# Attention, routed experts and a rational feed-forward on one core: expert stores without mutual waits, a branch hint for ScalarE, the conversion steps dealt out anew, the router's last part in another order

## The chip, the cores and the metric

The kernel runs on 1 core of a Trainium2 chip. The metric is device time in microseconds (us). Engines: TensorE (PE; PEld is its weight load), VectorE (DVE), ScalarE (ACT), GpSimd (POOL) and SyncE (SP), which only issues transfers here. Each takes its instructions in program order.

## The reference

- Chunked attention on q, k, v (4 batches, 8 heads, 768 positions, 64 wide): each chunk of 32 positions sees 8 memory keys, 16 positions to the left and 8 to the right. The result is x, 3072 tokens x 512.
- A mixture of experts: `logits = x @ w_gate + modality_bias[modality_id]`; each token goes to its best expert of 8; `out = gate * (relu(x @ w1[e]) @ w2[e])`, with 512 x 1024 and 1024 x 512 weights.
- A feed-forward stage: `h = x @ w_in` (2048 wide), `g = P(h) / (Q(h) + 1e-6)` with a cubic P and `Q = 1 + |b0||h| + |b1|h^2`, then `g @ w_out`.

All is float32; w_in, w_out, a and b arrive as float64.

## The kernel before, in words

Three stages follow each other on the PE. Attention (`attention`) walks 24 tiles of 128 tokens, writes x to a DRAM tensor `xd` and ends in `Router.second`. The experts (`moe`) work on units of 128 tokens of one expert: units 0, 1 and 2 (`EARLY`) one by one within `second`, then five quads of four units (units 3 to 22, `Q_FIRST` = 3), and unit 23 (`S_LAST`). The feed-forward stage (`moe2`) has 6 blocks of 512 tokens.

Numbers: a product of float32 values is made of three fp32r products, with a rounded part ("h") and a rest ("l") of each operand (hi x hi, hi x lo, lo x hi). `split_hi` (ACT) and `split_lo` (DVE) do this for expert weights, `prep_x` (4 PE transposes, an ACT copy, a DVE subtraction) for a unit's tokens, `prep_h` for a hidden block. Unit 0 uses plain float32 (`prep_h0`, `mm2_0`).

A quad, L1003 to L1047: for each of 8 blocks n of the hidden width, `mm1_quad(n)` (12 products of 512 columns), `relu_quad(n)` (ACT, then DVE L895), then `mm2_quad(n - 1)` (12 products). After `mm2_quad`, `at(n)` places other work: a conversion step (`filler`), loads of the next expert's weights, their splits (n = 5 and 6, in quads without a small unit), the gathers for the next quad. At n = 7 and behind it come the four `prep_x` of the next quad, the rest of the splits, and four `out`. Splits and weight loads run under a branch: only if the next quad has another expert. In this run they are taken at the ends of quads 1 and 2.

Quads 0 and 3 also carry a "small" unit of at most 32 tokens of another expert: its weights go to the raw buffers w1r and w2r (`load` at n = 0 and 1), its rows are gathered by POOL (`gather_small`, L783, behind the four stores of the quad before), transposed on the PE at n = 3 (L792, ahead of `mm2_quad(2)`), and multiplied at n = 3 and n = 4 (L800, L816).

Stores of results: `out` writes a row number (POOL, L872), scales the result (ACT L876 or DVE L874) into one of four buffers `xy` and lets POOL scatter 128 rows to the DRAM tensor `yd` (indirect store, L877). The framework orders accesses to the same tensor: as every scatter may touch any row of `yd`, each waits on POOL until the one before has landed. POOL's queue also issues the gathers (L753) and the stores of converted weights (L1175, L1176).

Conversion (`converter`): 32 pieces of w_in (16) and w_out (16) are narrowed from float64 and split, a step at a time. A step does `pair` of one piece (ACT and DVE L1172, L1173; for w_out two stores to `wod` through a buffer of two slots), the load of the piece after the next, and `bits` of the next (ACT L1114, DVE L1115 to L1118). The first step also loads piece 0. `filler` is called at n = 0 to 6 of each quad: 35 calls for 33 steps.

`Router.second` places the tokens: the matmuls into `tb` (L602) give each unit's row list `src_u` (L609, L611), from which POOL gathers the units' tokens; `bg` and the matmuls into `gp` (L639, L649) give the gates that `out` needs.

Behind unit 23 stands `if more` (L1074), a long body for odd distributions of tokens, which this run skips: every engine compares and branches past it. `mark_branch_hint_location` stands ahead of unit 23's second product.

Of the kernel before, what the change touches and what calls it, by code (L numbers as in the profile page):

```python
# [22 lines left out]
P = 128  # L23
# [269 lines left out]
EARLY = 2  # L293
QUAD = 4
QUADS = 5
Q_FIRST = EARLY + 1
# [4 lines left out]
class Router:  # L301
# [229 lines left out]
    def second(self):  # L531

        nc, V, ex = self.nc, self.nc.vector, self.ex
        n = self.N1
# [59 lines left out]
        last[1]()  # L594
        low()
        ex.relu(0)
        for i in range(1, 4):
            ex.split_lo(ex.w1r, ex.w1h, ex.w1l, i)
        for i in range(4):
            ex.split_hi(ex.w2r, ex.w2h, i)  # L600
        for t in range(NT):
            nc.tensor.matmul(tb, lhsT=self.at1[:, :, t] if t < n else at2[:, :, t - n], rhs=bt[:, :, t], start=(t == 0), stop=(t == NT - 1))  # L602
        for part in range(3):
            ex.mm1(1, part)
        ex.prep_h0(0, 0)
        ex.prep_h0(0, 1)
        f = self.wk.tile([P, 6, 32], F32, tag="df", name="f")

        V.tensor_scalar(out=f[:, 0], in0=tb, scalar1=0.0, scalar2=BIGI, op0=ALU.is_equal, op1=ALU.mult)  # L609
# [1 line left out]
        V.scalar_tensor_tensor(out=self.src_u[:, a], in0=tb[:, a], scalar=float(NT * P // 2), in1=f[:, 0, a], op0=ALU.add, op1=ALU.add)  # L611
        for s in range(EARLY, EARLY + 4):
            ex.gather(s)
        some = self.wk.tile([P, 32], F16, tag="rs", name="some")
        V.tensor_scalar(out=some, in0=tb, scalar1=0.0, scalar2=None, op0=ALU.not_equal)
        V.tensor_scalar(out=f[:, 1], in0=tb, scalar1=0.0, scalar2=-1.0, op0=ALU.is_gt, op1=ALU.mult)
# [11 lines left out]
        ex.load_w(Q_FIRST, 1)  # L628
        for step in (*rest[4:], *self.gates(n, NT), *self.gate_parts()):
            step()  # L630
        for i in range(4):
            ex.split_lo(ex.w2r, ex.w2h, ex.w2l, i)
        for part in range(3):
            ex.mm1(EARLY, part)
            if part < 2:
                ex.prep_h(1, part)
        bg = self.wk.tile([P, NT, 3, 32], F16, name="bg", bufs=1)
        SG = [P, NT, 3, 32]
        V.tensor_tensor(  # L639
            out=bg, in0=be.rearrange("p s t -> p t s")[:, :, None, :].to_broadcast(SG), in1=self.g16[:, :, :, None].to_broadcast(SG), op=ALU.mult,  # L640
        )
        ex.relu(EARLY)
        low = ex.prep_x(Q_FIRST, 0)
        ex.mm2(1, 0)
        low()
        ex.split_w(Q_FIRST, 1)
        gp = self.tp.tile([P, 3, 32], F32, tag="t", name="gp")
        for t in range(NT):
            nc.tensor.matmul(gp, lhsT=self.at1[:, :, t] if t < n else at2[:, :, t - n], rhs=bg[:, t], start=(t == 0), stop=(t == NT - 1))  # L649
        ex.mm2(1, 1)  # L650
        gs = self.wk.tile([P, 3, 32], F32, tag="df", name="gs")
        nc.scalar.copy(gs, gp)
        V.scalar_tensor_tensor(out=gs[:, 1], in0=gs[:, 2], scalar=1.0 / GP, in1=gs[:, 1], op0=ALU.mult, op1=ALU.add)
        V.scalar_tensor_tensor(out=self.ex.gate_s, in0=gs[:, 1], scalar=1.0 / GP, in1=gs[:, 0], op0=ALU.mult, op1=ALU.add)
        ex.out(0, ex.ys0)
        ex.out(1, ex.ys1)
        ex.load_w(EARLY, 2)
        ex.prep_x(Q_FIRST + 1, 1)()
        for g in range(2):
            ex.prep_h(EARLY, g)  # L660

    def slots(self, col, end, off, f, cnt):

# [40 lines left out]
class Experts:  # L704


    def __init__(self, nc, tc, ident, xd, yd, w1, w2, src_u, pos_u, out_u, gate_s):
        self.nc, self.tc, self.ident = nc, tc, ident
        self.xd, self.yd, self.src_u, self.pos_u, self.out_u, self.gate_s = xd, yd, src_u, pos_u, out_u, gate_s
        self.w1v = w1.rearrange("e (p k) f -> (e p) (k f)", k=4)  # L710
        self.w2n = w2
        self.hps, self.yps, self.hT = {}, {}, {}
        self.ctx = ExitStack()
        self.sp = self.ctx.enter_context(tc.tile_pool(name="shared", side="right", bufs=1))
        self.ps = self.ctx.enter_context(tc.tile_pool(name="shared_ps", side="right", bufs=4, space=PSUM))
        self.pa = [self.ps.tile([P, 512], F32, name=f"pa{i}", bufs=1) for i in range(2)]
        self.pvx = ExitStack()
        self.pv = self.pvx.enter_context(tc.tile_pool(name="a_pv", side="right", bufs=1, space=PSUM)).tile([P, 2, 512], F32, name="pv")
        self.xy = [self.sp.tile([P, D_M + 16], F32, name=f"xy{i}") for i in range(QUAD)]
        self.xg = [x[:, 0:D_M] for x in self.xy]  # L720
        self.w1r = self.sp.tile([P, 4, 1024], F32, name="w1r")
        self.w1h = self.sp.tile([P, 4, 1024], F32R, name="w1h")
        self.w1l = self.sp.tile([P, 4, 1024], F32R, name="w1l")
        self.w2r = self.sp.tile([P, 4, 1024], F32, name="w2r")
        self.e0 = self.sp.tile([1, 1], I32, name="e0")
        self.flags = self.sp.tile([1, 3, 32], I32, name="flags")
        self.sp.tile([P, 8], F32, name="pad_s")
        self.xT = {}
# [93 lines left out]
    def out_small(self, k, ps, y):  # L822
        nc, s = self.nc, NS - 1 - k
        nc.gpsimd.tensor_copy(y[0:SM, D_M:D_M + 1].bitcast(U32), self.out_u[0:SM, s:s + 1])
        for c in range(4):
            nc.scalar.activation(y[0:SM, P * c:P * c + P], ps[SM * c:SM * c + SM], func=AF.Copy, scale=self.gate_s[0:SM, s:s + 1])
        nc.gpsimd.indirect_dma_start(
            out=self.yd, out_offset=bass.IndirectOffsetOnAxis(ap=self.pos_u[0:SM, s:s + 1], axis=0), in_=y[0:SM, 0:D_M + 1], in_offset=None,
            bounds_check=NT * P - 1, oob_is_err=False,
        )  # L830

    def split_hi(self, raw, hi, i):
        self.nc.scalar.copy(hi[:, i], raw[:, i])
# [33 lines left out]
                    start=(i == 0 and w is self.w2h and n == 0), stop=(w is self.w2l and n == 7),  # L867
                )

    def out(self, s, y=None, ps=None, dve=False):  # L870
        nc, y, ps = self.nc, self.xy[s % QUAD] if y is None else y, self.pa[s % 2] if ps is None else ps
        nc.gpsimd.tensor_copy(y[:, D_M:D_M + 1].bitcast(U32), self.out_u[:, s:s + 1])  # L872
        if dve:
            nc.vector.tensor_scalar(out=y[:, 0:D_M], in0=ps, scalar1=self.gate_s[:, s:s + 1], scalar2=None, op0=ALU.mult)  # L874
        else:
            nc.scalar.activation(y[:, 0:D_M], ps, func=AF.Copy, scale=self.gate_s[:, s:s + 1])  # L876
        nc.gpsimd.indirect_dma_start(  # L877
            out=self.yd, out_offset=bass.IndirectOffsetOnAxis(ap=self.pos_u[:, s:s + 1], axis=0), in_=y[:, 0:D_M + 1], in_offset=None,
            bounds_check=NT * P - 1, oob_is_err=False,
        )  # L880

    def mm1_quad(self, n):
        ps = self.ps.tile([P, 512], F32, tag="t", name="hq")
# [91 lines left out]
def moe(nc, tc, ex, filler, rows):  # L975
# [3 lines left out]
    def quad(q):  # L979
# [10 lines left out]

        def at(n):

            if n < 7:
                filler()
            if k is not None and n < 2:
                ex.load(e, n + 1)
            if n in loads:
                layer, i = loads[n]
                ex.load_w(nxt[0], layer, range(i, i + 2))
            if n == part1:  # L1000
                ex.split_w(nxt[0], 1, range(2))
            if n == part2:
                ex.split_w(nxt[0], 2, range(2))  # L1003
            if n == (2 if k is None else 5):
                for c in nxt:
                    ex.gather(c)
# [44 lines left out]
    def first_y(t):  # L1051
        ps = ex.ps.tile([P, 4, P], F32, tag="t", name="yps") if t < 2 else ex.pb[t - 2].rearrange("p (k n) -> p k n", k=4)
        rows.prep(t, w1r[:, t, 0:D_M + 1], ps, rows.h, rows.l)

    ex.split_w(EARLY, 2)
    for t in (3, 2):
        ex.prep_x(Q_FIRST + t, t)()
    for q in range(QUADS):
        quad(q)
    ex.hs = ex.w2r[:, 0].rearrange("p (i j n) -> p i j n", i=2, j=4)  # L1060
# [6 lines left out]
        first_y(t)  # L1067
    ALL = (ET.PE, ET.Activation, ET.DVE, ET.Pool, ET.SP)
    more = nc.values_load(flags[0:1, 2, 0:1], engines=ALL, min_val=0, max_val=1)
    tc.mark_branch_hint_location("more", "LikelyTaken", engines=(ET.PE,))  # L1070
    for g in range(2):
        ex.mm2(S_LAST, g)
    ex.out(S_LAST)
    with tc.If(more == 1, label="more"):  # L1074
        for i in range(Q_FIRST, NN):
            if i == S_LAST or i < S_LAST and (i - Q_FIRST) % QUAD == 0:
                continue
            todo = nc.values_load(flags[0:1, 2, i:i + 1], engines=ALL, min_val=0, max_val=1)
            with tc.If(todo == 1):
                e = ex.expert(i)  # L1080
                for layer in (1, 2):
                    ex.load(e, layer)
                    ex.split_w(i, layer, always=True)
                ex.gather(i)
                ex.prep_x(i)()
                for part in range(3):
                    ex.mm1(i, part)
                ex.relu(i)
                ex.prep_h(i, 0)
                ex.prep_h(i, 1)  # L1090
                for part in range(2):
                    ex.mm2(i, part)
                ex.out(i)
        for t in range(4):
            rows.load(t, w1r[:, t, 0:D_M + 1])
        for t in range(4):
# [24 lines left out]
class Rows:  # L1121


    def __init__(self, nc, cp, rp, ident, yd):
        self.nc, self.ident, self.yd = nc, ident, yd
        self.out = cp.tile([P, NT], U32, name="out_rows")
        self.rp = rp

# [2 lines left out]
        self.l = self.rp.tile([P, NK, TB], F32R, tag="b", name="yl0")  # L1131

    def load(self, i, r):
        self.nc.sync.dma_start(out=r, in_=self.yd[i * P:(i + 1) * P, :])

    def prep(self, i, r, ps, h, l):
        nc = self.nc
# [8 lines left out]
def converter(nc, rows, w_in, w_out, wih, wil, wod):  # L1146
# [28 lines left out]
            nc.gpsimd.dma_start(out=wod[x, :, 0], in_=hi.bitcast(F32))  # L1175
            nc.gpsimd.dma_start(out=wod[x, :, 1], in_=lo.bitcast(F32))  # L1176

    n_done = [0]
    last = len(pieces)

    def step():
        n = n_done[0]
        if n > last:
            return False
        if n == 0:
            load(0)
        if n >= 1:
            pair(n - 1)
        if n + 1 < last:
# [173 lines left out]
def program(nc, tc, q, k, v, mod, wg_d, mbias, w1, w2, w_in, w_out, a, b, out):  # L1363
    with tc.manual_schedule(), ExitStack() as ctx:
# [19 lines left out]
        wih = [wp.tile([P, DF], F32R, name=f"wih{k}") for k in range(NK)]  # L1384
        wil = [wp.tile([P, DF], F32R, name=f"wil{k}") for k in range(NK)]
        rp = ctx.enter_context(tc.tile_pool(name="conv", reuse_waits="tile", bufs=1))
        rows = Rows(nc, cp, rp, ident, yd)
        step = converter(nc, rows, w_in, w_out, wih, wil, wod)
        moe(nc, tc, ex, step, rows)
        ex.ctx.close()  # L1390
# [51 lines left out]
```

## Time and profile before

| | us |
|---|---|
| median of 3 runs | 983.01 (979.91 to 986.11) |
| profiled execution, its own time | 982.91 |
| its span, first to last instruction | 980.9 |
| PE busy | 929.5 (95%) |
| DVE busy | 745.4 (76%) |
| ACT busy | 535.5 (55%) |
| POOL busy | 141.8 (14%) |

The profiled execution's time is its span and 2.0 us around it. In the trace the attention stage runs to about 110 us, `second` to 156 us, the quads from 156, 212, 261, 313 and 376 us, unit 23 to 435 us, and `moe2` from there. Times in rows are us from the span's start. A busy PE need not be at its peak: the column PEclk tells the granted clock, 1.00 being full speed.

### The profile page before, as it was taken

To read this page: it belongs to the slowest core of one execution; us is meant where nothing else is said; L and a number is where in the kernel's file an instruction comes from. 1 tells how busy PE (TensorE), PEld (TensorE's weight loads), DVE (VectorE), ACT (ScalarE), POOL (GpSimd) and SP (SyncE) were. 2 spreads that over 40 slices of the span, in tenths; PEclk is the share of its full clock that TensorE was granted. 3 is DMA by queue.
4 is the path that set the end of the run, shared out by engine and by line. 5 is a ranking of instruction groups with operands and counts; after the bars stand their busy time and mean duration, and the time that the engine had idled before them with its cause. 6 is when DMAs were issued, how large, how long until landed. Compare 5 with 4: busy or idle time off the path is not lost.

```text
span 980.9 us, 15489 instructions
## 1 busy us (share of the span) xinstructions
PE 929.5 (95%) x5749; PEld 754.0 (77%) x5749; DVE 745.4 (76%) x1235; ACT 535.5 (55%) x891; POOL 141.8 (14%) x207
## 2 busy tenths in 40 slices
PE   5998999999998599989999999999999999999997
PEld 4776667788786478877888888888888888888885
DVE  5777783465958356428998889989898898899885
ACT  2444533343626133227767677766776677766673
POOL 5111121022131333211000100100010010001001
PEclk9999999999999799999999999999999999999999
DMA  8999633448293854437120100101010000001001
GB/s 254 350 387 354 233 98 122 163 137 319 83 337 129 302 180 146 147 101 277 55 65 11 43 22 23 44 3 30 12 44 11 23 31 23 21 1 44 1 1 43
DMA packets 41498, 114.50 MB, mean 117 GB/s; under 512 B 6886, under 2 KB 6914, under 8 KB 41412
## 3 DMA queue, kind: packets, MB, share of 16 engines
q1 hardware_dynamic: 31252, 80.62, 24.5%
q0 software_dynamic: 10160, 32.79, 8.9%
q8 instruction: 46, 0.75, 0.3%
q14 instruction: 40, 0.33, 0.1%
HBM read 86.24 MB, written 27.41 MB: 116 GB/s over the span
## 4 chain that ended last, share of the span: by engine, by line
PE 53%; DVE 1%; ACT 0%; issue 0%; POOLq 0%; POOL 0%; ACTq 0%
PE a L1314 9%; PE h L1255 9%; PE a L1312 9%; PE a L1313 9%; PE h L1257 9%; PE h L1256 9%; PE yps L1140 1%; DVE q L1274 0%; DVE u L1287 0%; DVE q L1286 0%; DVE q L1285 0%; DVE gl L1297 0%; DVE u L1275 0%; ACT s L1267 0%; POOLq L1438 0%
## 5 line engine op out<-in xcount | busy, mean ns | idle before, releaser
L1255 PE MATMUL h<-yh,wih 128*128 128x512 f32 x384 | 152.4, 397 | 2.7 <-ACTq L1074 2.7
L1314 PE MATMUL a<-wo,gl 128*128 128x512 f32 x384 | 149.7, 390 | 1.3 <-DVE gl L1297 1.3
L1312 PE MATMUL a<-wo,gh 128*128 128x512 f32 x384 | 149.5, 389 | 0.7 <-ACT gh L1291 0.7
L1257 PE MATMUL h<-yh,wil 128*128 128x512 f32 x384 | 150.1, 391 | 0.0
L1256 PE MATMUL h<-yl,wih 128*128 128x512 f32 x384 | 150.1, 391 | 0.0
L1313 PE MATMUL a<-wo,gh 128*128 128x512 f32 x384 | 149.4, 389 | 0.0
L1267 ACT ACTIVATE s<-h 128x512 f32<-128x512 f32 x96 | 56.5, 589 | 83.9 <-PE h L1257 83.9
L1274 DVE SCALAR_TENSOR_TENSOR q<-s,ab,q 128x512 f32<-128x512 f32 x96 | 71.7, 747 | 32.8 <-ACT q L1268 32.8
L1255 PEld LDWEIGHTS h<-yh,wih 128*128 128x128 f32 x384 | 72.5, 189 | 17.7 <-ACTq L1074 3.1
L1291 ACT CAST gh<-u 128x512 fp32r<-128x512 f32 x96 | 59.9, 624 | 46.4 <-DVE u L1287 46.4
L1314 PEld LDWEIGHTS a<-wo,gl 128*128 128x128 f32 x384 | 72.1, 188 | 17.0 <-DVE gl L1297 2.1
L1312 PEld LDWEIGHTS a<-wo,gh 128*128 128x128 f32 x384 | 72.1, 188 | 16.1 <-ACT gh L1291 1.3
L1257 PEld LDWEIGHTS h<-yh,wil 128*128 128x128 f32 x384 | 72.4, 189 | 15.6
L1256 PEld LDWEIGHTS h<-yl,wih 128*128 128x128 f32 x384 | 72.6, 189 | 14.5
L1313 PEld LDWEIGHTS a<-wo,gh 128*128 128x128 f32 x384 | 72.1, 188 | 14.9
L1269 ACT ACTIVATE u<-h,ab 128x512 f32<-128x512 f32 x96 | 74.9, 780 | 0.0
L1287 DVE SCALAR_TENSOR_TENSOR u<-u,ab,q 128x512 f32<-128x512 f32 x96 | 72.1, 752 | 3.4
L1276 DVE SCALAR_TENSOR_TENSOR u<-u,ab,h 128x512 f32<-128x512 f32 x96 | 71.7, 747 | 3.4
L1285 DVE SCALAR_TENSOR_TENSOR q<-q,ab,s 128x512 f32<-128x512 f32 x96 | 71.7, 746 | 0.1
L1280 ACT ACTIVATE s<-q,ab 128x512 f32<-128x512 f32 x96 | 70.4, 733 | 1.2 <-DVE q L1274 0.2
L1286 DVE SCALAR_TENSOR_TENSOR q<-q,s 128x512 f32<-128x512 f32 x96 | 66.4, 692 | 3.3
L1324 POOL DMA_INDIRECT out<-o,out_rows x24 | 26.5, 1104 | 283.9 <-ACT o L1320 205.3
(293 smaller groups left out, 1784.0 us busy)
## 6 DMA issues: line engine op xcount, KB each, us to landing
v<-in_v SPq DMA_DIRECT2D x48, 260.0 KB, 5.7
w1r<-in_moe_w SPq DMA_DIRECT2D x20, 512.0 KB, 6.8
w2r<-in_moe_w SPq DMA_DIRECT2D x20, 512.0 KB, 7.3
wr<-in_moe_w_in SPq DMA_DIRECT2D x16, 512.0 KB, 3.9
wr<-in_moe_w_out SPq DMA_DIRECT2D x16, 512.0 KB, 4.3
wod<-wo POOLq DMA_DIRECT2D x32, 256.0 KB, 3.6
wo<-wod SPq DMA_DIRECT2D x16, 512.0 KB, 7.8
k<-in_k SPq DMA_DIRECT2D x48, 168.0 KB, 5.2
```

Of the source, the lines that this page charges most:

```text
L1255: nc.tensor.matmul(ps, lhsT=wih[k][:, sl], rhs=h[:, k], start=(k == 0), stop=False)
L1256: nc.tensor.matmul(ps, lhsT=wih[k][:, sl], rhs=l[:, k], start=False, stop=False)
L1257: nc.tensor.matmul(ps, lhsT=wil[k][:, sl], rhs=h[:, k], start=False, stop=(k == NK - 1))
L1269: A.activation(u, ps, func=AF.Identity, scale=a3, bias=a2)
L1274: V.scalar_tensor_tensor(out=q, in0=s, scalar=absb1, in1=q, op0=ALU.mult, op1=ALU.add)
L1276: V.scalar_tensor_tensor(out=u, in0=u, scalar=a1, in1=ps, op0=ALU.add, op1=ALU.mult)
L1280: A.activation(s, q, func=AF.Ln, bias=cb)
L1285: V.scalar_tensor_tensor(out=q, in0=q, scalar=cb, in1=s, op0=ALU.add, op1=ALU.mult)
L1287: V.scalar_tensor_tensor(out=u, in0=u, scalar=a0, in1=q, op0=ALU.add, op1=ALU.mult)
L1312: nc.tensor.matmul(ps, lhsT=gh[:, sl], rhs=wo[x][:, 0].bitcast(F32R), start=(x == 0), stop=False)
L1313: nc.tensor.matmul(ps, lhsT=gh[:, sl], rhs=wo[x][:, 1].bitcast(F32R), start=False, stop=False)
L1314: nc.tensor.matmul(ps, lhsT=gl[:, sl], rhs=wo[x][:, 0].bitcast(F32R), start=False, stop=(x == NF - 1))
```

## The change

Five edits. Scatters of `out` and `out_small` are declared independent of each other; reads of `yd`, and the scatters inside the skipped body, depend on all of them by hand. The branch hint names ACT beside the PE. The first conversion step only loads piece 0 and is called ahead of the quads; the call at n = 6 stays in quads 0, 3 and 4 alone. In `second`, `src_u` and the first gathers come ahead of most splits, and `bg`, the token transposes of units 6, 5, 4 and 3, the w2 rests and the first units' products are put in another order.

```diff
@@ Router.second
         ex.relu(0)
-        for i in range(1, 4):
-            ex.split_lo(ex.w1r, ex.w1h, ex.w1l, i)
-        for i in range(4):
-            ex.split_hi(ex.w2r, ex.w2h, i)
+        ex.split_lo(ex.w1r, ex.w1h, ex.w1l, 1)
         for t in range(NT):
             nc.tensor.matmul(tb, ...)
-        for part in range(3):
-            ex.mm1(1, part)
-        ex.prep_h0(0, 0)
-        ex.prep_h0(0, 1)
 ...
         for s in range(EARLY, EARLY + 4):
             ex.gather(s)
+        for i in range(2, 4):
+            ex.split_lo(ex.w1r, ex.w1h, ex.w1l, i)
+        for i in range(4):
+            ex.split_hi(ex.w2r, ex.w2h, i)
+        for part in range(3):
+            ex.mm1(1, part)
+        ex.prep_h0(0, 0)
+        ex.prep_h0(0, 1)
 ...
-        for i in range(4):
-            ex.split_lo(ex.w2r, ex.w2h, ex.w2l, i)
-        for part in range(3):
-            ex.mm1(EARLY, part)
-            if part < 2:
-                ex.prep_h(1, part)
         bg = ...
         V.tensor_tensor(out=bg, ...)
+        def x(*tiles):
+            for low in [ex.prep_x(Q_FIRST + t, t) for t in tiles]:
+                low()
+        def w2_lo(*pieces):
+            for i in pieces:
+                ex.split_lo(ex.w2r, ex.w2h, ex.w2l, i)
+        x(2)
+        ex.mm1(EARLY, 0)
+        ex.prep_h(1, 0)
+        w2_lo(0, 1)
+        ex.mm1(EARLY, 1)
+        ex.prep_h(1, 1)
+        x(3)
+        w2_lo(2)
+        ex.mm1(EARLY, 2)
         ex.relu(EARLY)
-        low = ex.prep_x(Q_FIRST, 0)
+        x(1, 0)
+        w2_lo(3)
+        ex.split_w(Q_FIRST, 1)
         ex.mm2(1, 0)
-        low()
-        ex.split_w(Q_FIRST, 1)
+        ex.prep_h(EARLY, 0)
         gp = ...            # 24 matmuls into gp
-        ex.mm2(1, 1)
 ...                         # gate_s from gp
         ex.out(0, ex.ys0)
+        ex.mm2(1, 1)
+        ex.prep_h(EARLY, 1)
         ex.out(1, ex.ys1)
         ex.load_w(EARLY, 2)
-        ex.prep_x(Q_FIRST + 1, 1)()
-        for g in range(2):
-            ex.prep_h(EARLY, g)
@@ Experts
+    def own_rows(self, d):
+        self.tc.declare_no_dep(d.ins, group="yd", reason="each column has its own rows")
+        self.tc.add_to_no_dep_group("yd", d.ins)
+        self.outs.append(d.ins)
+    def after_outs(self, d):
+        for x in self.outs:
+            self.tc.add_manual_dep(d.ins, x.name, ..., reason="rows of y")
-    def out(self, s, y=None, ps=None, dve=False):
+    def out(self, s, y=None, ps=None, dve=False, again=False):
 ...
-        nc.gpsimd.indirect_dma_start(out=self.yd, ...)
+        d = nc.gpsimd.indirect_dma_start(out=self.yd, ...)
+        (self.after_outs if again else self.own_rows)(d)
@@ moe
-            if n < 7:
+            if n < 6 or n == 6 and q in (0, 3, 4):
                 filler()
 ...
+    filler()
     ex.split_w(EARLY, 2)
-    for t in (3, 2):
-        ex.prep_x(Q_FIRST + t, t)()
 ...
-    tc.mark_branch_hint_location("more", "LikelyTaken", engines=(ET.PE,))
+    tc.mark_branch_hint_location("more", "LikelyTaken", engines=(ET.PE, ET.Activation))
@@ Rows
-        self.nc.sync.dma_start(out=r, in_=self.yd[i * P:(i + 1) * P, :])
+        self.after(self.nc.sync.dma_start(out=r, in_=self.yd[i * P:(i + 1) * P, :]))
@@ converter
-    n_done = [0]
+    n_done = [-1]
-        if n == 0:
+        if n < 0:
             load(0)
+            n_done[0] += 1
+            return True
```

## Rows read from the trace of the kernel before

**Rows 1.** Waits of PE: what for, us in total, times, longest.

```profile
PE xps L792 <- DMA xy<-xd,src_u: 10.3, 1, 10.3
PE xps L951 <- DVE hl L895: 3.8, 2, 1.9
PE h L1255 <- ACTq L1074: 2.7, 1, 2.7
```

**Rows 2.** Windows: length, busy us of each engine (instructions), PEclk, DMA share, GB/s.

```profile
313.00:376.00 63.00, 52.74 (x310) 42.22 (x309) 33.05 (x54) 21.22 (x40) 21.70 (x29) 0.89 0.63 218
456.00:974.00 518.00, 517.25 (x2317) 427.36 (x2316) 464.84 (x686) 355.67 (x590) 32.04 (x42) 1.00 0.09 31
```

**Rows 3.** Timeline of POOL, quad 3: start, us, operation, [idle before <- what ended it].

```profile
314.37 1.05 POOL L877 DMA_INDIRECT yd<-xy,pos_u  x1 [9.10 <-issue]
...
335.65 0.98 POOL L877 DMA_INDIRECT yd<-xy,pos_u  x1 [6.92 <-DMA yd<-xy,pos_u]
336.94 0.96 POOL L783 DMA_INDIRECT xy<-xd,src_u  x1 [0.30 <-issue]
```

**Rows 4.** Windows from small unit's transposes to its first product, quads 0 and 3.

```profile
177.69:181.22 3.53, 3.53 (x17) 2.73 (x16) 0.69 (x1) 0.80 (x2) 0.00 (x0) 1.00 0.77 306
...
339.70:345.56 5.86, 5.86 (x16) 4.35 (x16) 3.44 (x6) 1.88 (x4) 1.59 (x3) 0.52 0.84 289
```

**Rows 5.** Timeline of SP and PE: the small unit's w2 in quad 3.

```profile
323.48 2.22 SPq L765 DMA_DIRECT2D w2r<-in_moe_w  x4
...
353.34 1.96 PE L816 MATMUL syp<-w2r,xy 128*32 128x128 f32 x64
```

**Rows 6.** Transfers issued from 312 to 340 us: KB each, median us to landing.

```profile
w2r<-in_moe_w SPq DMA_DIRECT2D x4, 512.0 KB, 12.7
```

**Rows 7.** Windows from block 7's first product to the next quad, quads 0, 1, 2.

```profile
201.90:212.05 10.15, 10.15 (x53) 8.70 (x52) 6.37 (x11) 3.82 (x8) 1.71 (x4) 1.00 0.41 129
247.41:261.28 13.87, 11.98 (x53) 9.99 (x52) 13.27 (x18) 9.36 (x14) 0.00 (x0) 0.88 0.13 45
296.64:312.88 16.24, 12.18 (x53) 9.55 (x52) 14.59 (x21) 11.38 (x16) 2.88 (x5) 0.89 0.39 133
```

**Rows 8.** Timeline of DVE (quad 1, around n = 6) and of ACT (quad 2).

```profile
250.51 0.68 DVE L1173 TENSOR_TENSOR wil<-wr,wih 128x512 fp32r<-128x512 f32 x1
...
253.36 2.35 DVE L836 TENSOR_TENSOR w2l<-w2r,w2h 128x1024 fp32r<-128x1024 f32 x2
...
296.61 0.65 ACT L1172 CAST wo<-wr 128x512 fp32r<-128x512 f32 x1 [7.27 <-DMA wod<-wo]
```

**Rows 9.** Windows: router's last part; end of unit 23 to the first activation of `moe2`.

```profile
127.00:157.00 30.00, 26.08 (x133) 18.77 (x131) 19.50 (x45) 9.38 (x19) 4.72 (x7) 1.00 0.48 157
435.18:442.39 7.21, 4.49 (x14) 3.61 (x15) 0.00 (x0) 0.69 (x1) 2.81 (x8) 0.76 0.57 173
```

**Rows 10.** Timeline of POOL, PE and DVE in the router's last part.

```profile
120.46 3.48 DVE L836 TENSOR_TENSOR w1l<-w1r,w1h 128x1024 fp32r<-128x1024 f32 x3
...
125.01 1.00 POOL L753 DMA_INDIRECT xy<-xd,src_u  x1 [20.69 <-DVE f L616]
...
128.57 0.72 PE L951 MATMUL xps<-ident,xy 128*128 128x128 f32 x4 [1.40 <-DVE f L694]
...
142.00 4.31 DVE L639 TENSOR_TENSOR bg<-be,g 128x2304 f16<-128x2304 f16 x1
```

**Rows 11.** Line 1074: sequencer, instruction, duration ns min/median/max, first and last start.

```profile
L1074 DVEq EVENT_SEMAPHORE  x2: 21/21/21, 434.5 to 434.6; - x2
L1074 PEldq EVENT_SEMAPHORE  x2: 51/51/51, 435.2 to 435.4; - x2
L1074 ACTq EVENT_SEMAPHORE  x2: 17/17/17, 437.8 to 437.9; - x2
...
L1074 PEldq COMPARE_BRANCH  x1: 4147/4147/4147, 430.9 to 430.9; - x1
...
L1074 ACTq COMPARE_BRANCH  x1: 50/50/50, 435.3 to 435.3; - x1
```

More of the change, by code (lines that the diff above doesn't have):

```diff
@@ L711, in __init__ @@
         self.w2n = w2
-        self.hps, self.yps, self.hT = {}, {}, {}
+        self.hps, self.outs = {}, []
         self.ctx = ExitStack()
@@ L826, in out_small @@
             nc.scalar.activation(y[0:SM, P * c:P * c + P], ps[SM * c:SM * c + SM], func=AF.Copy, scale=self.gate_s[0:SM, s:s + 1])
-        nc.gpsimd.indirect_dma_start(
+        self.own_rows(nc.gpsimd.indirect_dma_start(
             out=self.yd, out_offset=bass.IndirectOffsetOnAxis(ap=self.pos_u[0:SM, s:s + 1], axis=0), in_=y[0:SM, 0:D_M + 1], in_offset=None,
             bounds_check=NT * P - 1, oob_is_err=False,
-        )
+        ))
+    def own_rows(self, d):
[4 more added lines that the diff above has]
+        for x in self.outs:
+            self.tc.add_manual_dep(d.ins, x.name, mybir.DependencyInfo(mybir.DependencyClass.Sync, mybir.DependencyReason.DATA), reason="rows of y")
     def split_hi(self, raw, hi, i):
@@ L876, in out @@
             nc.scalar.activation(y[:, 0:D_M], ps, func=AF.Copy, scale=self.gate_s[:, s:s + 1])
-        nc.gpsimd.indirect_dma_start(
+        d = nc.gpsimd.indirect_dma_start(
             out=self.yd, out_offset=bass.IndirectOffsetOnAxis(ap=self.pos_u[:, s:s + 1], axis=0), in_=y[:, 0:D_M + 1], in_offset=None,
@@ L1092, in moe @@
                     ex.mm2(i, part)
-                ex.out(i)
+                ex.out(i, again=True)
         for t in range(4):
@@ L1121, with __init__ @@
 class Rows:
-    def __init__(self, nc, cp, rp, ident, yd):
-        self.nc, self.ident, self.yd = nc, ident, yd
+    def __init__(self, nc, cp, rp, ident, yd, after):
+        self.nc, self.ident, self.yd, self.after = nc, ident, yd, after
         self.out = cp.tile([P, NT], U32, name="out_rows")
@@ L1386, in program @@
         rp = ctx.enter_context(tc.tile_pool(name="conv", reuse_waits="tile", bufs=1))
-        rows = Rows(nc, cp, rp, ident, yd)
+        rows = Rows(nc, cp, rp, ident, yd, ex.after_outs)
         step = converter(nc, rows, w_in, w_out, wih, wil, wod)
```

## The prediction

> **What bounds the kernel.** First the waits of the PE, since it is busy for 929.5 of 980.9 us: the reader is to see one wait of 10.3 us, for the rows of a small unit, then waits for DVE rests (hl) and for ACT at line 1074 [rows 1]. Then the windows: from 456 to 974 us the PE is busy for 517.25 of 518 us at full clock, so nothing can be won in the feed-forward stage; quad 3 has 10 us of idle PE and a granted clock of 0.89 [rows 2]. Wherever the PE waits, it may lose twice, by the idle time and by products at half clock (1.2 in place of 2.4 GHz) behind it. So each wait is priced against a like stretch without one.
>
> **Stores, quad 3.** POOL issues the four stores of quad 2 from 314.37 on, each after the landing of the one before; the last goes out at 335.65 after 6.92 us of idleness, and only then, at 336.94, the gather of the small unit [rows 3]. The PE, in order, sits before that unit's transposes until 339.70 and then works at clock 0.52 up to the unit's first product: 5.86 us, against 3.53 us for the same stretch of quad 0, where nothing was late [rows 4]. The loss is 10.3 + (5.86 - 3.53) = 12.6 us. Without the mutual waits a store follows the last at about 0.98 us plus the gap of 0.30 us that the gather shows [rows 3]: four from 314.37 are out by 319.5, the gather starts near 320 instead of 336.94, and the PE wants its rows at 339.7 - 10.3 = 329.4 us. That leaves 9 us to land; it took 2.8 us on an emptier queue (336.94 to 339.70). Upper bound of the gain: all 12.6 us. What is late next is this transfer itself, and the unit's second weights. These go out from 323.48 on and need a median of 12.7 us [rows 5, 6], with four transfers issued within 2.2 us: the last lands near 338.4, while the product that reads them, at 353.34 [rows 5], comes 12.6 us sooner, at 340.7. The slack is 2.3 us, and the stores of converted weights, now freed on POOL, come on top: two pieces, 1.05 MB, less the two row stores (0.53 MB) that leave earlier. At the 218 GB/s for a share of 0.63 [rows 2], so 346 GB/s at full share, the net 0.52 MB is 1.5 us and all of the 1.05 MB 3.0 us: late by at most 0.7 us. Lower bound: a gather as slow as those weights, 12.7 us, is 3.3 us late, and with 3 us for the weights the gain is 6.3 us. I take 12.4, because the nearest row, the gather's 2.8 us, is far below the 9 us that it has.
>
> **Conversion steps and stores, ends of quads 1 and 2.** From block 7's first product to the next quad takes 10.15 us where no splits fall, 13.87 and 16.24 us where they do [rows 7]. In quad 1 DVE is the bound there: 13.27 of 13.87 us busy. The call at n = 6 puts `pair` and `bits` on it, from 250.51 to the w2 splits at 253.36 [rows 8]: 2.85 us, which go. The rest of DVE's work is 10.42 us; with the 0.60 us that it was idle, 11.0. So the gain lies between 13.87 - 11.0 = 2.9 and 13.87 - 10.15 = 3.7 us: 3.3. In quad 2 ACT had also stood for 7.27 us, until 296.61, before a `pair` whose buffer was still to be stored to `wod` [rows 8], since POOL's queue stood behind row stores; its later work, and DVE's, ran late into this stretch. With the stores free that wait should go too, and the stretch should be quad 1's, about 10.6 us: a gain of 5.6. Bounds: 16.24 - (14.59 - 2.85 + 0.6) = 3.9, if the late work stays, and 16.24 - 10.15 = 6.1. The two steps taken out there go to n = 5 and 6 of quad 4, which has no splits; the call ahead of the quads only issues a load on SP. Both cost nothing while DVE has room, as in quad 0's end, with the same lack of splits: 6.37 of 10.15 us busy [rows 7]. If that cover were gone, a step would cost 2.85 us.
>
> **Router's last part.** Between 127 and 157 us the PE is idle for 30.00 - 26.08 = 3.9 us [rows 9]. 1.40 us of it stand before unit 2's transposes at 128.57, put down to a DVE instruction; I read it as the gather, issued at 125.01 [rows 10], 3.6 us before. `src_u` now comes after one w1 split instead of three (3.48 us for three from 120.46 on [rows 10]), so the gathers go out 2/3 x 3.48 = 2.3 us sooner and that wait goes. The rest stands before the gates' matmuls (behind `bg`, 142.00, 4.31 us [rows 10]) and before quad 0 (its last tokens' rests). Both producers move ahead: `bg` before the four w2 splits, the transposes of units 6, 5, 4 and 3 between unit 2's products. No instruction is added on PE or DVE; the gathers pass nothing on POOL, SP has one load sooner. What is now late is w2's rest, by `bg` and by the rests of tokens put among the splits; in front of its reader the PE has unit 2's 24 products and five sets of transposes. Bounds: all 3.9; or, if `bg` is passed on in full to unit 1's product, 3.9 - 4.3 = -0.4. I take 3.6, since the PE's work there outlasts DVE's.
>
> **Branch hint.** The PE's last wait in [rows 1] is for ACT: ACT branches at 435.3 and its semaphores follow only at 437.8, while those of DVE and of the PE, which has the hint, are set by 434.6 and 435.4 [rows 11]. From the end of unit 23 to ACT's first pass of `moe2` go 7.21 us, at a clock of 0.76 [rows 9]; twelve products need 12 x 0.23 = 2.8 us (517.25 us over 2317 recorded products [rows 2], a few of which are missing), and ACT's last pass before, 0.69 us [rows 9], may still hold a buffer. That leaves 3.7 us, at most 4.1 without that pass (2.4 sooner, and 4.5 - 2.8 = 1.7 at full clock). Below: nothing, if the hint does nothing; or a loss, if a hinted branch takes what the PE's took, 4.15 us [rows 11], from 435.3 on: 439.4, 1.6 us later than now. I take 3.6: the PE's branch had run since 430.9 and its end coincides with the last products, while ACT passes the place of the hint some 4 us ahead of its branch. The Trainium skill, "Runtime: NRT & Kernel Launch", section "Instruction fetch mechanics", says that instructions are prefetched in sequence only, and that a taken branch out of the window waits for a fetch; by that rule this term would be 0. The trace agrees in that ACT waits 2.5 us; of a hint on ACT it shows nothing.
>
> **Sum.** 12.4 + 3.3 + 5.6 + 3.6 + 3.6 = 28.5. The profiled execution took 982.9 us (span 980.9), 0.1 from the median of the runs. The forecast is 982.9 - 28.5 = 954.4 us. All upper bounds together (12.6 + 3.7 + 6.1 + 3.9 + 4.1 = 30.4) give 952.5; the runs of before spread by 3.1 us to either side.
>
> **Rivals.** *The stores still wait.* If the declared independence is lost somewhere, the gather stays late. Then 12.4 go, and quad 2 keeps ACT's wait: 3.3 + 2.9 (the step alone) + 3.6 + 3.6 = 13.4, 969.5 us. For it speaks only that such a declaration has no row here; `out` stores of the feed-forward stage use the same one. 5%.
> *Transfers collide.* Stores, converted weights and 4 MB of the small unit's weights now meet, at a DMA share of 0.84 already [rows 4]: 3.3 + 3.0 us come back by the bounds above, 960.5. Against it: the slacks of 9 and 2.3 us. 7%. The Trainium skill, "DMA: Bandwidth & Descriptors", section "Issuing engines are not separate DMA queues", says that transfers of all issuers interleave on the same 16 engines, which speaks for this rival; the 12.7 us [rows 6] agree with it.
> *The hint brings nothing.* 3.6 come back: 958.0. 15%; this is the page's rule above.
> *Slower: SP's queue.* Reads of `yd` now depend on some 26 stores by hand. Their first one in `moe2` stands in SP's queue ahead of nine of the 16 loads of `wo`. If SP were held there, the PE would run on until the tenth step, (3 x 12 + 7 x 24) x 0.23 = 47 us into the stage, and each later us would be lost. To undo 28.5 us SP must be held for some 76 us; at 100 us the time is 1007. Nothing in the rows holds a store's landing for that long (6.9 us [rows 3]). 2%.
>
> **Numbers.** The forecast holds with 70%, within 950 to 958. The range takes in collision, the idle hint, lower bounds of two terms at once and the runs' spread: 948 to 966. A change under 1% (9.8 us) is about what a measurement of this kernel can't tell from none. Faster by over 1% (under 973.2): forecast, hint, collision, still-waiting stores less a few: 0.95. Within 1%, if still-waiting stores meet the other terms' lower ends: 0.03. Slower: 0.02.
>
> **What would show it.** In the new profile: the four stores of a quad 1.3 us apart, the gather at L783 within 8 us of quad 3's start, no PE wait at L792, no ACT wait for `wod` stores; both split stretches of 10 to 11 us; the gathers near 122.7 and no waits of over 0.5 us from there to quad 0; ACT's semaphores of the skipped body within 1 us of its branch; PEclk at 1.00 from 160 us on. Wrong would be: a new wait at L800 or L816, a PE wait for hl in the same places, or unit 1's second product waiting for w2's rest.

## The result, and the profile after

The changed kernel took 957.79 us (median of 4 runs, 954.94 to 959.04), the kernel before 984.56 us on the same chip: a ratio of 0.9721, 95% interval 0.9662 to 0.978. Forecast were 954.4 us, range 948 to 966. The profiled execution took 958.5 us, its span 956.5, against 980.9 before: 24.4 us less. Where they lie is worked out from the starts of stages in the PE's timeline of each kernel (us; "to tb": first unit's transposes to the matmuls into `tb`; "end": block 7's first product to the next quad; each stage is one trace):

```
          attention  to tb  tb-quad 0  quad 0  quad 1 (end)    quad 2 (end)    quad 3  quad 4, unit 23  moe2
before      109.08    9.98    36.04    56.95   49.23 (13.87)   51.60 (16.24)   63.51       61.51       543.00
after       106.37   11.46    31.54    56.40   45.54 (10.16)   47.00 (10.91)   57.32       59.28       541.59
gain          2.7    -1.5      4.5      0.5      3.7             4.6             6.2         2.2         1.4
```

The code of the first stage is the same; it took 106.4 to 114.0 us in all the traces, so kernels are compared by stages below, or from `tb` on (before 861.8, after 838.7 us).

The PE's waits after (line waited at, for what, us in total, times, longest), of those that answer to [rows 1]. Lines 792, 800, 816, 951 and 1255 of before are 804, 812, 828, 974 and 1279 now:

```profile
PE sps L812 <- ACT xy L805: 3.3, 1, 3.3
...
PE h L1279 <- ACTq L1096: 0.9, 1, 0.9
PE xps L804 <- DMA xy<-xd,src_u: 0.8, 1, 0.8
...
PE pb L930 <- DVE hl L918: 0.7, 2, 0.4
```

The last of these lines had its like in before, where [rows 1] don't show it:

```profile
PE pb L907 <- DVE hl L895: 2.3, 2, 2.2
```

The 10.3 us for the small unit's rows are down to 0.8. The waits for `hl` at the transposes (3.8 us) are gone, those at the products (L907, L930 now) fell from 2.3 to 0.7 us. The wait behind the branch fell from 2.7 to 0.9. The first line is new: a wait at what was L800, which the prediction had named as a sign of being wrong. Windows of after (columns as in [rows 2]): the ends of quads 1 and 2, then the router's last part:

```profile
241.15:251.31 10.16, 10.16 (x54) 8.70 (x52) 8.94 (x11) 6.82 (x10) 0.00 (x0) 1.00 0.00 0
287.40:298.31 10.91, 10.53 (x54) 8.69 (x52) 10.56 (x14) 8.36 (x12) 0.00 (x0) 1.00 0.03 14
```

```profile
118.00:148.00 30.00, 30.00 (x173) 23.18 (x172) 26.35 (x62) 13.63 (x24) 5.43 (x6) 1.00 0.33 101
```

Quad 1's end, bound by DVE in [rows 7], is now all PE; quad 2's lacks 0.4 us of it; from `tb` to quad 0 the PE no longer stops. POOL's timeline at quad 3 (start, us, instruction, idle time before it and its releaser), which answers to [rows 3]; quad 3 starts at 298.31:

```profile
301.15 1.05 POOL L899 DMA_INDIRECT yd<-xy,pos_u  x1 [16.63 <-DVE xy L896]
...
306.58 1.27 POOL L899 DMA_INDIRECT yd<-xy,pos_u  x1 [0.28 <-POOL xy L894]
308.15 1.09 POOL L795 DMA_INDIRECT xy<-xd,src_u  x1 [0.30 <-issue]
309.25 0.59 POOL L1197 DMA_DIRECT2D wod<-wo  x1
...
311.13 0.54 POOL L1198 DMA_DIRECT2D wod<-wo  x1
```

The last of the four stores goes out 5.4 us behind the first (before: 21.3), and the gather 9.8 us into the quad, 24 before. Yet quad 3 shortened by 6.2 us, not 12.4. ACT's and the PE's timelines show what came in its place:

```profile
309.93 0.59 ACT L917 ACTIVATE hh<-hq 128x512 fp32r<-128x512 f32 x1
316.87 0.65 ACT L1194 CAST wo<-wr 128x512 fp32r<-128x512 f32 x1 [6.35 <-DMA wod<-wo]
321.19 0.66 ACT L1136 ACTIVATE wf<-wr 128x512 f32<-128x512 f32 x1 [3.68 <-DMA wr<-in_moe_w_out]
321.75 0.58 ACT L917 ACTIVATE hh<-hq 128x512 fp32r<-128x512 f32 x1
322.23 0.26 ACT L805 COPY xy<-xps 128x128 f32<-128x128 f32 x1
```

```profile
315.66 0.66 PE L804 MATMUL xps<-ident,xy 32*128 32x32 f32 x4 [0.76 <-DMA xy<-xd,src_u]
...
322.54 3.52 PE L812 MATMUL sps<-w1r,xy 128*32 128x256 f32 x32 [3.26 <-ACT xy L805]
```

The small unit's rows are transposed at 315.66, but ACT copies them only at 322.23: ahead of that copy in its queue stand two passes of the conversion, one waiting 6.35 us for a buffer whose stores to `wod` had not landed, one 3.68 us for raw weights of the feed-forward stage. The PE stops for 3.26 us, and the unit's 32 products then take 3.52 us. The windows of these microseconds (next to last columns: granted clock, DMA share, GB/s):

```profile
310.31:314.31 4.00, 4.00 (x20) 3.30 (x19) 2.59 (x5) 0.21 (x1) 1.36 (x3) 1.00 1.04 376
...
318.31:322.31 4.00, 0.97 (x5) 0.46 (x3) 0.92 (x2) 1.12 (x3) 0.58 (x2) 1.00 1.04 414
322.31:326.31 4.00, 3.77 (x33) 1.68 (x34) 2.41 (x4) 0.33 (x3) 0.00 (x0) 0.57 1.05 403
```

All DMA engines are busy for 16 us (a share of 1.00 is all of them; the shares printed run a little above it), and behind the wait the clock is granted at its lower level for most of 4 us.

### The profile page after: what moved, and what is told of

It reads as the page before. It is cut to its first block, busy times and chain, and to the rows that moved or that the text cites. A ratio compares the mean times of both kernels' runs of the same rounds, so it can differ in the third digit from the quotient of the medians.

```text
span 956.5 us, 15489 instructions
## 1 busy us (share of the span) xinstructions
PE 923.9 (97%) x5749; PEld 749.6 (78%) x5749; DVE 745.1 (78%) x1235; ACT 535.2 (56%) x891; POOL 142.4 (15%) x207
## 4 chain that ended last, share of the span: by engine, by line
PE 54%; DVE 2%; ACT 0%; issue 0%; POOLq 0%; POOL 0%; ACTq 0%
PE a L1338 9%; PE a L1336 9%; PE a L1337 9%; PE h L1279 9%; PE h L1281 9%; PE h L1280 9%; PE yps L1162 1%; DVE q L1298 0%; DVE u L1311 0%; DVE q L1309 0%; DVE q L1310 0%; DVE gl L1321 0%; DVE u L1299 0%; ACT s L1291 0%; POOLq L1462 0%
```

## Experiments

**One part at a time**, each put alone into the kernel before: four kernels, one run each. The kernel before took 994.68 us on that chip, in one run of which no trace is kept; the expected totals start from the 982.9 us of the first chip. So the stages are read, against those of before in its one trace.

The stores' independence alone (`own_rows` and `after_outs`, nothing else of the change):

> The kernel before with independent row stores alone. Theory, parts that add: quad 2 loses ACT's wait for the wod buffer and comes to quad 1's length of 49.2 us (51.6 before), quad 3 falls from 63.5 to about 57.3 us, and nothing else moves: some 8.7 us less in all, 974 us. Rival, the stores and the step at n = 6 hide each other in quad 2: quad 2 stays above 51 us as long as the step at n = 6 is there, and the whole gives 6 us, 977 us.

976.82 us. Quad 3 went from 63.5 to 54.5 us, and the PE waited 2.03 us for the same copy, not for the rows. Quad 2 stayed at 51.1, as the rival said, its end at 15.68, though ACT's wait for `wod` of [rows 8] was gone. From `tb` on: 851.8, a gain of 10.1.

The conversion steps alone:

> The kernel before with the conversion steps dealt out anew, and nothing else. Theory, parts that add: the end of quad 1 (block 7 to the next quad) falls from 13.9 to 10.2 us, that of quad 2 from 16.2 to about 13.4 us, since ACT still waits for the wod buffer there, and quad 3 keeps its 63.5 us: 6.5 us less in all, 976 us. Rival: the end of quad 2 comes to 11 us without help from the stores: 9 us less, 974 us.

983.05 us. Ends of quads 1 and 2: 11.05 and 11.97 us, and here too ACT's wait for `wod` in quad 2 is gone, with the stores still chained. Either edit takes that wait away, and only the missing step shortens the end by much. Quad 3, which was to keep its 63.5 us, grew to 66.0; the PE's waits in its first 30 us:

```profile
PE xps L792 <- DMA xy<-xd,src_u: 11.9, 1, 11.9
```

The router's order alone:

> The kernel before with the new order in the router's last part alone. Theory: the stretch from the matmuls into tb to quad 0's first product falls from 36.0 to 31.5 us as in the changed kernel, all other stages stay: 978.4 us. Rival, the step that was left ahead of the quads in the changed kernel has a part in it: the stretch stays above 33 us.

982.86 us. From `tb` to quad 0 31.57 us as in after, the PE without a gap:

```profile
127.00:157.00 30.00, 30.00 (x158) 22.92 (x157) 21.60 (x53) 10.02 (x20) 4.99 (x7) 1.00 0.49 156
```

Quads 2 and 4 were 2.3 and 3.9 us longer than in the trace of before, quads 1 and 3 2.0 and 1.9 us shorter; from `tb` on 859.5 us, a gain of 2.4.

The hint alone:

> The kernel before with the branch hint for ACT alone. Theory: ACT's semaphores follow its branch by 0.7 us instead of 2.5, the PE waits 0.9 us instead of 2.7 for the feed-forward stage and has full clock there: 3.6 us less, 979.3 us. Rival, an instruction fetch that only runs in sequence: ACT's 2.5 us stay, 982.9 us.

990.17 us. ACT's sequencer at the branch (duration in ns, then first and last start), to be set against [rows 11]:

```profile
L1074 ACTq EVENT_SEMAPHORE  x2: 17/17/17, 446.5 to 446.6; - x2
...
L1074 ACTq COMPARE_BRANCH  x1: 69/69/69, 445.8 to 445.8; - x1
```

From branch to semaphores 0.7 us, 2.5 before; block 7 of quad 4 to the first product of `moe2` 23.96 us, 25.70 before; `moe2` 541.60, 543.00 before. The hint is worth 1.7 + 1.4 = 3.1 us. But quads 1 and 2, whose code is that of before, took 50.8 and 53.9 us, so the time from `tb` on was 862.3, no gain.

**What holds quad 3.** Theory A: POOL's queue, where the `wod` stores stand behind row stores and gather. Theory B: full DMA engines, whoever issues. First the `wod` stores issued by SP:

```diff
-            nc.gpsimd.dma_start(out=wod[x, :, 0], in_=hi.bitcast(F32))
-            nc.gpsimd.dma_start(out=wod[x, :, 1], in_=lo.bitcast(F32))
+            nc.sync.dma_start(out=wod[x, :, 0], in_=hi.bitcast(F32))
+            nc.sync.dma_start(out=wod[x, :, 1], in_=lo.bitcast(F32))
```

> The changed kernel, with the stores of converted weights into `wod` issued on SP's queue in place of POOL's. Theory A (in quad 3, ACT stands 6.35 us at the buffer of the converted pieces, because their stores wait on POOL behind row stores and the gather, and this holds up ACT's rests for the small unit): the wait of ACT for `wo` goes to under 1 us, the PE's wait of 3.3 us for the small unit's rests goes, and quad 3 takes 52 to 54 us in place of 57.3; the whole about 954. Theory B (the DMA engines are full in these 15 us, whoever issues): ACT still waits 3 us or more for `wod` or for the raw weights, and quad 3 takes 56 to 58 us; the whole 957 to 960.

970.57 us, from `tb` on 843.1 (838.7 in after); quad 3 59.7. ACT's waits in its first 32 us, then the PE's:

```profile
ACT wf L1136 <- DMA wr<-in_moe_w_out: 12.1, 3, 6.4
```

```profile
PE sps L812 <- ACT xy L805: 2.8, 1, 2.8
```

The wait for `wod` went, one for raw weights took its place (12.1 us, 7.2 in after), and the PE stands nearly as long as in after (2.8 for 3.3 us). That quad 3 is even longer, above the 56 to 58 us of theory B, lies at its end (13.89 us, 10.80 in after), where the PE waits 1.9 us for tokens of the next quad. So A alone falls: without its wait ACT is held as long by the next one. SP's order changed too, since the stores now stand ahead of loads, but the load that ACT waits for longest went out only 1.3 us later in the quad (318.34, 308.44 in after) and its data came 10.8 us behind that, 12.8 in after. Then half of the small unit's weights in quad 3 left out:

```diff
-                ex.load(e, n + 1)
+                ex.load(e, n + 1, range(4) if q == 0 else range(2))
```

> The changed kernel, with half of the small unit's weights of quad 3 not loaded (4 of 8 pieces, 2 MB of 4 MB; the products read what lay there before, so the output of that unit is wrong). Theory B (the DMA engines are full): the loads of raw weights and the `wod` stores land sooner, ACT waits under 3 us in all in the quad's first 15 us, the PE's wait for the rests falls under 1 us, and quad 3 takes 52 to 54 us. Theory A (POOL's order): ACT still waits some 5 to 6 us for `wod`, as its stores still go out behind row stores and the gather, and quad 3 takes 56 to 57.5 us.

960.1 us, from `tb` on 831.9. With 2 MB less on the engines the PE's wait for the copy is gone, and quad 3 takes 51.6 us at full clock:

```profile
305.61:357.21 51.60, 51.02 (x312) 41.06 (x310) 33.56 (x54) 21.70 (x40) 21.72 (x30) 1.00 0.66 226
```

ACT still waited 5.3 us for `wod`, as A said and B did not, but the 3.68 us for raw weights behind it were gone, and the copy came in time. So both waits hold ACT in after; with less traffic the first is 1.0 us shorter and the second gone. The same from the other side: no conversion in the first two blocks of quad 3, two steps more in quad 0.

```diff
-            if n < 6 or n == 6 and q in (0, 3, 4):
+            if n < 6 and not (q == 3 and n < 2) or n == 6 and q in (0, 3, 4):
                 filler()
+            if q == 0 and n in (1, 2):
+                filler()
```

> The changed kernel without the conversion steps of the first two blocks of quad 3; the two steps are taken in quad 0 instead (after its second and third block there is one step more). Both theories: the conversions' loads, passes and stores are gone from the start of quad 3, so the PE does not wait for the small unit's rests, quad 3 takes 51 to 53 us in place of 57.3 and its granted clock is 1.00; quad 0 at most 1 us longer; the whole about 953. If quad 3 stays above 56, neither the converted weights nor their stores are what held it, and what is left is the small unit's own weights behind the row stores.

965.07 us, from `tb` on 841.2. Windows of quads 0 and 3:

```profile
153.68:217.20 63.52, 58.05 (x337) 46.21 (x336) 34.62 (x59) 22.62 (x42) 10.28 (x14) 0.97 0.43 146
311.37:362.38 51.01, 50.95 (x311) 41.01 (x310) 28.23 (x44) 19.55 (x36) 19.31 (x26) 1.00 0.69 229
```

Quad 3 won 6.3 us, as expected; quad 0, where I had allowed 1 us, lost 7.1: its small unit now met the conversions, and the PE waited 5.2 us for the same copy. That the copy would also be in time if it stood ahead of the conversion's passes in ACT's queue is likely from the timeline, but was not tried.

**The change without free stores** (`own_rows` no longer called):

> The changed kernel with one part undone: the stores of expert results wait for each other again. The prediction's price of this part is 12.4 us (stores, quad 3) and up to 2.7 us of quad 2's end: quad 3 back at 63 to 66 us with a wait of 10 us of the PE for the small unit's rows, the whole about 969. If the part is worth only what the stages of the two kernels show (6.2 us in quad 3), quad 3 takes 63 us and the whole is 964; if quad 2's wait comes back too, 967.

981.08 us; quads 2 and 3 50.3 and 65.1 us, with 11.9 us of PE wait for the rows. From `tb` on 853.7 against 838.7: 15.0 us, in one run. The prediction's rival "the stores still wait" has nearly this price (969.5 - 954.4 = 15.1), but by luck: it takes 12.4 us from quad 3 and 2.7 from quad 2, the traces give 7.8 and 3.3, and the other 3.9 us lie in stages that the rival leaves alone.

**A better place for the two steps.** The three variants here leave the conversion out of quad 3's first two blocks. Two steps into quad 4, doubled at n = 3 and n = 4:

> The changed kernel without the conversion steps of the first two blocks of quad 3; the two are taken in quad 4 instead, in the middle of its fourth and fifth blocks, where there is no small unit and the DMA share is 0.16 to 0.67. If it is the meeting of conversions and the small unit's weights on full DMA engines that costs quad 3 its 6 us, quad 3 takes 51 to 52 us in place of 57.3, quad 0 stays at 56.4 (it took 63.5 where the two steps were added there), quad 4 grows by at most 1 us, and the time is 5 to 6 us (0.5 to 0.6%) below the changed kernel on the same chip. If the loss only follows the steps wherever they go, quad 4 grows by 4 us or more and nothing is won.

968.42 us (median of 6), ratio 0.9791, interval 0.9761 to 0.982. Beside it the changed kernel again:

> The changed kernel itself once more, beside the others on the same chip: a ratio to the kernel before of 0.970 to 0.978, and stages as in its first trace, within 1 us but for the attention, which moved by some us from run to run: the router's last part 31.5 us, quads 45.5, 47 to 48, 57 and 59.3 us, with the PE's wait for the small unit's rests at the start of quad 3 again (2 to 4 us).

964.0 us, ratio 0.9749, interval 0.9726 to 0.9773; 838.9 us from `tb` on, the PE's wait 3.2 us: the same picture as in the first trace. In the variant quad 4 grew by 6.3 us (PE waits of 1.8 and 1.2 us for a block's own passes on DVE and ACT, which stand among those of the conversion, clock 0.74 behind), and quad 3 did not shorten (56.3 us): the PE waited 3.3 us for the small unit's rows. One step in quad 1, one in quad 4:

> As the kernel whose two steps went to quad 4, but one of them goes to quad 1 (in the middle of its third block) and one to quad 4. Quad 1's loads of raw weights meet a DMA share of 0.96 to 0.99 in its second to fourth block, but no small unit. If it is the small unit's rests that make a late conversion costly, quad 1 stays at 45.5 to 46.5 and quad 3 at 51 to 52 us; if a full DMA share is enough, quad 1 grows by 2 us or more.

960.12 us (one run), from `tb` on 839.6: no gain on the 838.9. Windows of quads 1 and 3:

```profile
206.61:258.75 52.14, 48.69 (x210) 39.73 (x208) 33.74 (x53) 21.50 (x33) 9.81 (x12) 0.93 0.57 191
305.80:357.13 51.33, 50.95 (x311) 41.02 (x310) 27.99 (x44) 19.56 (x36) 19.02 (x26) 1.00 0.69 227
```

Quad 1 grew by 6.6 us, without any small unit: there the doubled step itself is what costs, in waits of the PE of 1.8 and 1.7 us for the block's own passes on DVE and ACT and a lower clock behind them (0.93 over the quad). The single doubled step of quad 4 cost nothing (59.28). So one there, and one behind all others, at n = 7:

```diff
-            if n < 6 or n == 6 and q in (0, 3, 4):
+            if n < 6 and not (q == 3 and n < 2) or n == 6 and q in (0, 3, 4) or n == 7 and q == 4:
+                filler()
+            if q == 4 and n == 4:
                 filler()
```

> The changed kernel without the conversion steps of quad 3's first two blocks; one is taken as a second step at quad 4's fifth block, where it cost nothing in an earlier run (59.28 us), the other as the last step of all at quad 4's eighth block, where DVE is busy for 0.27 of 8 us. If the conversions on full DMA engines are quad 3's loss, quad 3 takes 51 to 52 us, quad 4 59.3 to 60.5, the other stages as in the changed kernel, and the ratio to the kernel before is 0.967 to 0.971, against the changed kernel's 0.975 on one chip and 0.972 on another. If not: quad 3 over 55 us, or quad 4 over 62, and a ratio of 0.973 or more.

960.08 us (median of 6), ratio 0.9761, interval 0.9725 to 0.9796, from `tb` on 838.1: not better than the change. Quad 4 was free of loss (59.28), but quad 3 took 57.6 us. The PE's wait there, and the gather's own sequencer:

```profile
PE xps L804 <- DMA xy<-xd,src_u: 4.2, 1, 4.2
```

```profile
L795 POOLq EVENT_SEMAPHORE  x1: 5326/5326/5326, 308.4 to 308.4; - x1
```

The gather writes a buffer that the row stores of quad 2 read, so it waits for a landing. With no conversion step ahead of them in SP's queue the small unit's weights go out earlier, here ahead of the row stores, at 302.29 against 303.36; the stores then land 10.4 to 12.0 us after their issue (3.5 to 8.8 in after, where the weights start at 305.36). In the two kernels without these steps whose quad 3 took 51 us the weights start 0.2 to 0.3 us behind the first store, and the gather's semaphore takes 0.04 us. That the order of these two issues decides is read from these traces and that of the two steps in quad 4 (weights 1.1 us ahead of the first store, the semaphore 3.8 us); it wasn't tried by itself.

## Why the prediction was right, and where it was not

**Stores, quad 3: mis-sized, 12.4 against 6.2 us.** The mechanism held: free stores, gather early, hardly a wait for the rows. But of the signs named ahead, the stores went out 1.8 us apart and not 1.3, the gather 9.8 us into the quad and not within 8, ACT did wait for `wod`, the clock fell, and the new wait at L800 came. What failed is the sentence on what is late next, "this transfer itself and the small unit's second weights". Neither was: the gather landed in 7.5 us and cost 0.76. Late was ACT's copy of the transposed rows, because conversion passes ahead of it waited for the same full DMA engines. I had priced the conversion's traffic as a delay of the second weights (up to 3 us) and left out its hold on ACT, which is in order. The lost 6.2 us: 0.76 + 3.26 of waits, 3.52 - 1.9 = 1.6 for products at the lower clock (1.93 us for the same 32 products in the run with half the weights), and 0.65 at the quad's end; sum 6.3. The lower bound of 6.3 us had the right size by another cause, which is luck.

Nor is all of the shortfall the stores' own: alone they gave 9.0 us in this quad (63.5 to 54.5), undone in the change 7.8. The moved conversion steps, of which the prediction says that they cost nothing, lengthened it by 2.5 us alone (63.5 to 66.0; 61.6 to 63.5 in the three kernels with the code of before there). Which of the other edits takes what in the change wasn't separated.

The rival "transfers collide" is what happened in this stage, at its price; the profiled run still came out at 958.5 (median of the runs 957.8), not 960.5, since other stages gave 0.9 more than forecast and the first stage, which the change leaves alone, 1.2. The Trainium skill, "DMA: Bandwidth & Descriptors", section "Issuing engines are not separate DMA queues", lets transfers of all issuers share 16 engines. The run with the `wod` stores on SP agrees with it: ACT's wait only changed its buffer.

**Quad 1's end: right**, 3.7 for 3.3 (the upper bound). The size rests on one trace of before: in the four kernels that keep the step (before and the stores, the order, the hint alone) this end took 11.9 to 15.4 us, without the step 10.2 to 11.6 (after, the steps alone, the change without free stores). **Quad 2's end: right in size**, 5.3 for 5.6, by a reason that is half wrong: freeing the stores alone left the end at 15.68 us, the step alone brought 11.97, and ACT's wait for `wod` was gone in both. So the work of the step made this end long, not that wait. In the change without free stores the end is 14.78: there ACT waits 5.9 us for raw weights, until 1.1 us into the end; with the steps alone a like wait of 4.9 us is over just ahead of the end. So a late transfer may count there, by another buffer; this is read from two traces, not shown.

**Router: 4.5 for 3.6**, above my upper bound of 3.9. The idle PE time went from 36.04 - 32.46 = 3.6 us to none, as forecast; the same products, back to back, also took 0.9 us less (31.54 busy). Moving `bg` and the transposes cost nothing in this stretch, alone and in the change.

**Hint: 3.1 for 3.6.** ACT's branch in after:

```profile
L1096 ACTq EVENT_SEMAPHORE  x2: 17/17/17, 414.8 to 414.9; - x2
...
L1096 ACTq COMPARE_BRANCH  x1: 69/69/69, 414.1 to 414.1; - x1
```

The PE's wait fell by 1.8 us only, since ACT's last pass ahead of the branch still ends late; the rest is the clock of `moe2`'s first products, 0.63 before and 1.00 after. The Trainium skill, "Runtime: NRT & Kernel Launch", section "Instruction fetch mechanics", says that prefetch is purely sequential and that a taken branch out of the window waits for a fetch; it names no hint, and by it alone this term would be 0. With a hint the traces differ: 0.7 us in place of 2.5, in after and with the hint alone. The rivals of the idle hint and of SP's queue fell.

**Sum.** From `tb` on the stages gave 23.2 of the 28.5 us: 6.2 short in quad 3, 0.9 over elsewhere. The first stage gave 1.2 more in this trace. One by one the parts gave 10.1, 1.5, 2.4 and -0.5 us from `tb` on, 13.5 in all, together 23.2. The difference doesn't lie in quad 3, where the parts gave 9.7 us and the change 6.2, but in quad 4 (the parts lost 4.9, 3.9 of it with the order alone; the change won 2.2), quad 2 (0.1 against 4.6) and quad 0 (a loss of 1.5 against a gain of 0.5). Its cause stays open, and part of it may be that each stage is one trace: in the three kernels whose quads 1 and 2 have the code of before (before, the order alone, the hint alone) these took 47.3 to 50.8 and 51.6 to 53.9 us.

## What to carry to other kernels

When a late transfer is brought forward, ask not only whether it lands in time but what each engine between it and its user has queued ahead, and what those instructions wait for: an engine in order passes on the wait of work that nobody is in a hurry for. On full DMA engines the wait moved here from buffer to buffer when another engine issued; less traffic in that stretch removed it, and so did, in two of four placements, traffic at another time. A place that looks idle by its busy shares has to be tried: none of the four placements won time in all.

## What the hardware showed that was not expected

- A hint on ACT brought its first instruction behind a skipped body from 2.5 to 0.7 us after the branch, while the branch of the PE's weight-load queue, hinted in every kernel, shows 2.9 to 4.5 us in the traces ([rows 11] and the other kernels).
- A second conversion step in one block cost 6.6 us in quad 1 (DMA share 0.96 to 0.99 around it in after) and nothing in quad 4 (0.61 to 0.67), but two such in neighbouring blocks of quad 4 cost 6.3 us. That the DMA share makes the difference isn't shown.
- The matmuls from the first unit's transposes to `tb` took 9.97 or 11.5 to 12.2 us with the same products there. The granted clock goes with it: 1.00 in that stretch of before, 0.85 in after, 0.71 with the hint alone (12.1 us); why it fell stays open.
